# Moving weight conversion behind the recurrence's own work in the first seven steps of a gated-linear-attention and FFN kernel

## The chip, the cores and the metric

One core of a Trainium2 chip. The core has TensorE (PE, matrix products), VectorE (DVE), ScalarE (ACT), GpSimd (POOL) and SyncE (SP, which issues most DMAs). Each runs its own list of instructions in order, and they wait for one another through semaphores. The metric is device time of one execution in microseconds (us), as the median of runs.

## The reference

A recurrent attention block feeds a feed-forward block. The attention inputs q, k, v and alpha have shape (4, 8, 768, 48): batch, heads, sequence, head width.

```python
state = np.zeros((B, H, D, D), dtype=np.float32)
for t in range(S):
    state = alpha[:, :, t, :, None] * state + np.einsum('bhd,bhe->bhde', k[:, :, t], v[:, :, t])
    y[:, :, t] = np.einsum('bhd,bhde->bhe', q[:, :, t], state)
...
x = attn_out.transpose(0, 2, 1, 3).reshape(B * S, H * D)   # 3072 x 384
a = x @ w1          # 384 x 1024
b = x @ w2
h = a * b @ w3      # 1024 x 1024
out = h @ w_out     # 1024 x 384
```

The feed-forward weights arrive as float64; attention inputs and the result are float32.

## The kernel before, in words

**Chunks.** The 3072 tokens are 24 chunks of 128 (four batches of six chunks). Inside a chunk the recurrence is written as matrix products: the logarithm of alpha (`la`, `logs`) is summed along the chunk by a product with a triangular matrix (`decays`, L286, or L289 from chunk 10 on), exponentials of the sums (`e`) scale k and q (`decayed`, L302, on VectorE, tile `qk`), TensorE transposes them (`transposed`, L324; ScalarE copies the result, `qkT`, L326), products of the two give scores (`scores`, L364), and VectorE masks them (`ms`, L367). `attend_state` (L384) and `attend` (L390) make the output from the carried state and from the masked scores; `outer` (L336) adds a chunk's keys and values to the state, with a sum on VectorE (L344, L346); `advance` scales the state on GpSimd every second chunk. The result x is copied by ScalarE (L394) and stored to DRAM (`xd`).

**Weights.** Float64 words are loaded as pairs of 32-bit integers (tile `raw`) and rebuilt as float32 by hand in `to_fp32`. For w1 and w2 there are twelve blocks of 128 x 512, each a generator (`load_gates`) that is taken on in pieces: a fetch issues the block's DMA, and then four calls of `convert(1)` do the rest:

- first: `rest` (L200) and `power` (L205) on ScalarE, two integer operations (L201, L204) on VectorE
- second: three operations on VectorE (L207, L208, L210)
- third: the high part `w` (L217) on ScalarE
- fourth: the low part (L219) on VectorE; for the first six blocks the third part `m` is left to `third`, two products on TensorE (L232, L233) and a copy on ScalarE (L234)

`convert(steps, ahead)` first sees to it that up to `ahead` blocks are fetched.

**Gates.** Groups of three chunks give tiles of 384 tokens. `split_x` splits x into three parts (L412 on ScalarE, L413 and L414 on VectorE), and a gate is 18 products for each of w1 and w2 (L420) over these parts and the weights' parts. Gates of group 0 are put into `fill` in step 6, and `run` takes pieces of them into steps from 7 on, between the attention's own work. After the loop come the remaining gates, the folding of w3 and w_out, and the final products; they are not touched here.

**The loop and its order.** A loop over n = 0 to 24 traces, for each step: stores and loads of later chunks, `attend_state(n - 1)`, `scores(n)`, `transposed(n + 1)`, at n = 6 the first `split_x`, conversion, `advance(n)`, `attend(n - 1)`, `outer(n)`, `third`, gates, conversion, `decayed(n + 2)`, `logs(n + 4)`, conversion, gates, `decays(n + 3)`, conversion, gates. A scheduler turns this into one list for each engine. It goes by the order of tracing and by its own estimates of when things are ready. `after_marks(names)` adds an order: what is traced inside the block comes after the marked instruction, on that instruction's own engine. Marks are `qkT` (ScalarE's copy, L326), `qk` (VectorE's product, L302), `ms` (VectorE's second mask, L367), `e` (ScalarE's second exponential) and `x3` (VectorE's last split of x, L414). The lists are then fixed: an engine whose next instruction waits does nothing else.

SP's queue holds loads of all chunks, the weight blocks and stores of x. Up to eight of its DMAs are outstanding; each issue waits for the DMA eight issues before.

"Chunk c" below is a chunk, "block" a weight block (one to twelve), and "step" is n.

Of the kernel before, what the change touches and what calls it, by code (L numbers as in the profile page):

```python
# [48 lines left out]
def kernel(  # L49
# [18 lines left out]
    N = B * NCH  # L68
# [34 lines left out]
    def bank():  # L103
        return ps.tile([C, 512], FP32, tag="bank", name="bank")
# [3 lines left out]
    def after_marks(*names):  # L108
        stack = ExitStack()
        for x in names:  # L110
            stack.enter_context(tc.issue_after(mark[x]))
        return stack
# [16 lines left out]
    def load_a(n):  # L129
        if n < N:  # L130
            st["a", n] = inp.tile([C, H, D], FP32, tag="ac", name="ac")
            nc.sync.dma_start(out=st["a", n], in_=rows(alpha, n))  # L132

    def load_kq(n):
        if n >= N:
            return
        st["kq", n] = inp.tile([C, 2, H, D], FP32, tag="kq", name="kq")
        nc.sync.dma_start(out=st["kq", n][:, 0], in_=rows(k, n))  # L138
        nc.sync.dma_start(out=st["kq", n][:, 1], in_=rows(q, n))  # L139

    def load_v(n):
        if n < N:
            st["v", n] = vs[n % len(vs)]
            nc.sync.dma_start(out=st["v", n][:, :, 0:D], in_=rows(v, n))
# [91 lines left out]
    def fetch(ahead=3):  # L236
        while weights and len(begun) < ahead:
            begun.append(weights.popleft())
            next(begun[-1])

    def convert(steps, ahead=3):

        for _ in range(steps):
            fetch(ahead)
            if not begun:
                return
            x = begun.popleft()
            try:
                next(x)
                begun.appendleft(x)  # L250
            except StopIteration:
                pass
# [4 lines left out]
    def store():  # L257

        while later:
            dst, src = later.popleft()  # L260
            nc.sync.dma_start(out=dst, in_=src)
# [18 lines left out]
    def decays(n):  # L280
        if n >= N:
            return
        lc = bank()[:, 0:DM]
        la = st.pop(("la", n))
        if n < LATE:
            nc.tensor.matmul(lc, sums[:, n % 2].bitcast(FP32), la, start=True, stop=True)  # L286
        else:
            for i in range(2):
                nc.tensor.matmul(lc, sums[:, n % 2], la[:, i], start=(i == 0), stop=(i == 1))  # L289

        e = st["e", n] = work.tile([C, 2, DM], FP32, tag="e", name="e", bufs=3)
        nc.scalar.activation(e[:, 0], lc, AF.Exp, scale=-1.0)
        mark["e", n] = nc.scalar.activation(e[:, 1], lc, AF.Exp).ins  # L293
        if n in ends:
            nc.gpsimd.dma_start(out=ends[n][0:1], in_=e[0:1, 0])
        if n + 1 in ends:
            nc.gpsimd.dma_start(out=ends[n + 1][1:2], in_=e[C - 1:C, 1])
        load_ends(n)
# [6 lines left out]
    def load_ends(n):  # L305
        if n not in ends:
            return
        with nc.allow_non_contiguous_dma(reason="single values to partitions"):
            for i in range(2):
                nc.gpsimd.dma_start(out=decs[n // 2 % 2][ds(DP * i, D)].rearrange("d m j -> d (m j)"),  # L310
                                    in_=ends[n].rearrange("m (j i d) -> i d (m j)", i=2, d=D)[i])

    def transposed(n):
        if n >= N:
            return
        qk = qks[n % 3]
        qkT = work.tile([C, 2, NP, C], FP32, tag="qkT", name="qkT")

        tp = [bank().rearrange("p (i j c) -> p i j c", i=2, j=NP) for _ in range(2)]
        for i in range(2):  # L320
            for j in range(NP):
                for half in range(2):
                    s = ds(DP * half, DP)
                    nc.tensor.transpose(tp[half][:, i, j, :], qk[s, i, 2 * j:2 * j + 2, :], ident[s, s])  # L324
        for half in range(2):
            mark["qkT", n] = nc.scalar.copy(qkT[:, :, :, ds(DP * half, DP)], tp[half]).ins  # L326
        st["qkT", n] = qkT
# [30 lines left out]
    def scores(n):  # L358
        qkT = st["qkT", n]
        sc = [bank().rearrange("p (j c) -> p j c", j=NP) for _ in range(2)]  # L360
        for j in range(NP):
            for i in range(2):
                r = ds(DP * i, D)
                nc.tensor.matmul(sc[i][:, j, :], qkT[r, 0, j, :], qkT[r, 1, j, :], start=True, stop=True)  # L364
        ms = work.tile([C, 2, NP, C], FP32, tag="ms", name="ms")
        for i in range(2):
            masked = nc.vector.tensor_tensor(ms[:, i].bitcast(I32), sc[i].bitcast(I32), keep_bc, op=ALU.bitwise_and)  # L367
        ends_of_part1[0] = mark["ms", n] = masked.ins
        st["ms", n] = ms
# [3 lines left out]
    def attend_state(n):  # L373
        qkT = st.pop(("qkT", n))

        y = [bank()[:, 0:HP * C].rearrange("p (j c) -> p j c", c=C) for _ in range(2)]
        st["y", n] = y, [(half * HP + j, i, y[i][ds(DP * half, DP), j, :])
                         for j in range(HP) for i in range(2) for half in range(2)]  # L380
        if n % NCH:
            for j, i, to in st["y", n][1]:
                r = ds(DP * i, D)
                nc.tensor.matmul(to, Ts[n % 2][r, j, :], qkT[r, 1, j, :],  # L384
                                 start=(j % HP == 0), stop=False, skip_group_check=True)
# [18 lines left out]
    def load_x(g, queue=nc.sync):  # L404
        st["xT", g] = xp.tile([C, KM, TG], FP32, tag="xT", name="xT")
        queue.dma_start(out=st["xT", g], in_=xd[g].rearrange("(k p) t -> p k t", p=C))

    def split_x(g, i):
        x = st.pop(("xT", g))
        t = tr[i].tile([C, 3, KM, TG], FP32R, tag="x3", name="x3")  # L410
        st["x3", g] = t
        nc.scalar.activation(t[:, 0], x, AF.Copy, scale=1.0 - 2.0 ** -13)  # L412
        nc.vector.tensor_sub(t[:, 1], x, t[:, 0].bitcast(FP32))  # L413
        mark["x3"] = nc.vector.scalar_tensor_tensor(t[:, 2], t[:, 0].bitcast(FP32), -1.0 - 1.0 / P, x,  # L414
                                                    op0=ALU.mult, op1=ALU.add).ins
# [73 lines left out]
    def gate(g, f):  # L489
        yield from (late_gate if late else early_gate)(g, f)  # L490
# [105 lines left out]
    begin = {4 + 4 * g: (g, range(FH if g < 4 else KF)) for g in range(5)}  # L596
    loads = {8: 1, 11: 2, 15: 3, 19: 4}

    for n in range(N + 1):
        store()  # L600
        if n in loads:
            load_x(loads[n])
        load_v(n + AHEAD - 1)
        load_a(n + 5)
        load_kq(n + AHEAD)
        if n:
            attend_state(n - 1)
        if n < N:
            scores(n)
        transposed(n + 1)  # L610
        if n - 2 in begin:
            g, tiles = begin[n - 2]
            with after_marks(("ms", n), ("qkT", n + 1)):
                split_x(g, 0)
            fill.extend(gate(g, f) for f in tiles)
        pieces = (0, 3, 3, 2)[(n - 6) % 4] if n > 5 else 0
        if n == 0:
            with after_marks(("qkT", 0)):
                logs(2)
            decays(2)  # L620
            with after_marks(("e", 2)):
                logs(3)
        early, ready = n < 7, len(thirds)
        behind = after_marks(*[("qkT", n + 1)] * (n < N - 1), *[("qk", n + 1)] * early, *["x3"] * (n - 2 in begin))
        if n < N - 2:
            with behind:
                convert(2 if n == 0 else 1, 2 if n == 0 else 3 if n < 8 else 4)
        advance(n)
        if n:
            attend(n - 1)  # L630
        outer(n)
        third(ready)
        run(pieces > 0)
        if early:
            with after_marks(("qkT", n + 1), ("qk", n + 1)):
                convert(1)
        with after_marks(*[("ms", n)] * (n < 3)):
            decayed(n + 2)
        logs(n + 4)
        if n == 4:  # L640
            load_x(0)
        convert(early and n > 2)
        run(pieces > 1)
        decays(n + 3)
        if n < N - 2:
            convert(early or n % 3 == 0, 3 if n < 8 else 4)
        run(pieces > 2)
        if n == N - 3:
            while begun:
                convert(1)  # L650
            weights.extend(load_out(j) for j in range(KF))
            fetch(4)
# [91 lines left out]
```

## Time and profile before

| | us |
|---|---|
| median of 3 runs (480.33 to 480.93) | 480.89 |
| profiled execution, its own time | 478.61 |
| its span | 476.8 |
| PE busy in the span | 458.3 (96%) |
| DVE busy | 356.3 (75%) |
| ACT busy | 282.1 (59%) |
| POOL busy | 73.1 (15%) |

The span is the time from the first to the last instruction of the profiled execution; its own time has 1.8 us around that. A busy share is an average over stages with different limits. The first 64 us hold steps 0 to 6 and the start of step 7, with PE, DVE, ACT and DMA all at work; later stages are products almost alone. By stretches, PE is busy 3.50 of the first 10 us, 8.06 of the next, then 9.75, 7.36, 9.94, 8.02 and 8.98, and all 10 from 70 to 80 us.

Start times that the text uses, from the trace in order of time:

| | start, us |
|---|---|
| scores (L364) of chunks 1 to 8 | 18.91, 25.41, 31.70, 40.74, 45.71, 50.55, 58.35, 71.4 |
| products qk (L302) of chunks 3 to 8 | 22.78, 33.46, 39.73, 44.34, 50.82, 57.88 |
| raw blocks two, four, five, six landed | 29.38, 37.83, 45.76, 52.48 |
| first gate products (L420) | 64.27 |

### The profile page before, as it was taken

The numbers are of one execution on the slowest core, as the hardware profiler recorded it, in microseconds if no ns is written. First come the engines' busy times: TensorE is split into PE (matmuls) and PEld (weight loads), VectorE is DVE, ScalarE is ACT, GpSimd is POOL, SyncE is SP. The second block draws the span as 40 slices with busy tenths as digits, with TensorE's granted clock in tenths as the row PEclk, the third lists the DMA queues.
The fourth block names the chain that finished last, engine by engine and source line by source line (L and its number), as shares of the span: only waits on it lengthen the run. The fifth ranks groups of instructions, "written<-read, shape, count | busy, mean of one in ns | idle before, by whom it ended". The sixth has DMA issues, their size and how long they took to land.

```text
span 476.8 us, 10002 instructions
## 1 busy us (share of the span) xinstructions
PE 458.3 (96%) x3836; PEld 435.2 (91%) x3836; DVE 356.3 (75%) x576; ACT 282.1 (59%) x556; POOL 73.1 (15%) x140
## 2 busy tenths in 40 slices
PE   4879899999999999999999999999999999999996
PEld 2658589899899999999999999999999999999996
DVE  2769888886988988999998888745642876666761
ACT  4667766866758555898876666644545433333330
POOL 3321231112302310212331101202010100000000
PEclk9888889999999999999999999999999999999999
DMA  9999999999999964657775333122105965555511
GB/s 171 178 200 220 241 211 212 229 234 211 197 216 206 210 202 133 200 170 234 242 216 209 109 124 100 50 84 90 44 36 157 261 189 169 164 170 172 177 51 49
DMA packets 153583, 80.29 MB, mean 168 GB/s; under 512 B 104480, under 2 KB 145568, under 8 KB 153536
## 3 DMA queue, kind: packets, MB, share of 16 engines
q1 hardware_dynamic: 148016, 65.22, 56.8%
q0 software_dynamic: 5520, 14.43, 9.5%
q8 instruction: 30, 0.49, 0.5%
q14 instruction: 17, 0.14, 0.1%
HBM read 57.58 MB, written 22.06 MB: 167 GB/s over the span
## 4 chain that ended last, share of the span: by engine, by line
PE 87%; DMA 5%; SPq 3%; DVE 2%; ACT 1%; issue 1%; DVEq 0%; ACTq 0%
PE bank L420 70%; PE bank L364 5%; PE bank L390 4%; DMA raw<-in_moe_w_dram 4%; PE bank L384 2%; PE bank L324 2%; SPq L139 2%; PE bank L336 1%; PE bank L522 1%; PE bank L289 1%; DMA ac<-in_alpha_dram 1%; SPq L138 1%; SPq L132 1%; PE bank L286 1%; DVE ms L367 0%
## 5 line engine op out<-in xcount | busy, mean ns | idle before, releaser
L420 PE MATMUL bank<-x,w 128*128 128x384 f32 x1152 | 210.9, 337 | 0.0
L420 PEld LDWEIGHTS bank<-x,w 128*128 128x128 f32 x1152 | 200.4, 188 | 1.3 <-issue 0.7
L420 PE MATMUL bank<-w3o,ab 128*128 128x384 f32 x576 | 100.2, 336 | 0.0
L420 PEld LDWEIGHTS bank<-w3o,ab 128*128 128x128 f32 x576 | 99.9, 188 | 0.0
L445 ACT ACTIVATE bank<-bank 128x384 f32<-128x384 f32 x98 | 46.7, 477 | 43.6 <-PE bank L420 43.3
L429 ACT ACTIVATE t<-bank 128x384 f32<-128x384 f32 x62 | 30.6, 494 | 62.3 <-PE bank L420 60.1
L495 POOL DMA_DIRECT2D abd<-ab x46 | 26.9, 584 | 132.8 <-DVE ab L481 125.2
L481 DVE TENSOR_TENSOR ab<-bank,r 128x384 f32<-128x384 f32 x45 | 24.9, 552 | 23.4 <-ACT bank L445 18.6
L551 DVE TENSOR_TENSOR ab<-abl,ab 128x1024 fp32r<-128x1024 f32 x24 | 29.4, 1224 | 13.6 <-ACT ab L550 13.5
L550 ACT ACTIVATE ab<-abl 128x1024 fp32r<-128x1024 f32 x24 | 25.5, 1061 | 20.9 <-PE bank L420 19.2
L326 ACT COPY qkT<-bank 128x512 f32<-128x512 f32 x48 | 26.1, 591 | 19.0 <-PE bank L324 19.0
L367 DVE TENSOR_TENSOR ms<-bank,keep 128x512 int32<-128x512 int32 x48 | 31.4, 683 | 7.8 <-PE bank L364 7.8
L420 PE MATMUL bank<-wo,w3T 128*128 128x384 f32 x192 | 35.9, 334 | 0.0
L420 PEld LDWEIGHTS bank<-wo,w3T 128*128 128x128 f32 x192 | 33.5, 188 | 0.0
L364 PEld LDWEIGHTS bank<-qkT 48*128 48x128 f32 x384 | 25.7, 204 | 7.0 <-issue 4.2
L431 DVE SCALAR_TENSOR_TENSOR o<-bank,t 128x384 f32<-128x384 f32 x24 | 13.4, 557 | 24.0 <-issue 15.6
L364 PE MATMUL bank<-qkT 48*128 48x128 f32 x384 | 30.7, 304 | 0.4 <-ACT qkT L326 0.4
L552 DVE SCALAR_TENSOR_TENSOR ab<-ab,abl 128x1024 fp32r<-128x1024 f32 x24 | 29.2, 1217 | 0.0
L302 DVE TENSOR_TENSOR qk<-kq,e 128x768 f32<-128x768 f32 x24 | 23.0, 958 | 8.2 <-ACT e L293 8.1
L390 PE MATMUL bank<-ms,v 128*64 128x128 f32 x384 | 28.3, 293 | 0.0
L205 ACT ACTIVATE power<-power,rebias 128x512 uint32<-128x512 uint32 (+1 forms) x36 | 25.1, 701 | 4.1 <-DVE power L204 3.8
L200 ACT ACTIVATE rest<-raw 128x512 f32<-128x512 uint32 (+1 forms) x36 | 23.3, 650 | 7.1 <-DMA raw<-in_moe_w_dram 7.1
(80 smaller groups left out, 573.3 us busy)
## 6 DMA issues: line engine op xcount, KB each, us to landing
raw<-in_moe_w_dram SPq DMA_DIRECT2D x28, 512.0 KB, 5.2
abl<-abd SPq DMA_DIRECT2D x24, 512.0 KB, 4.6
abd<-ab POOLq DMA_DIRECT2D x46, 192.0 KB, 3.1
xT<-xd POOLq DMA_DIRECT2D x9, 576.0 KB, 4.5
ac<-in_alpha_dram SPq DMA_DIRECT2D x24, 192.0 KB, 4.7
kq<-in_k_dram SPq DMA_DIRECT2D x24, 192.0 KB, 5.4
kq<-in_q_dram SPq DMA_DIRECT2D x24, 192.0 KB, 4.4
v<-in_v_dram SPq DMA_DIRECT2D x24, 192.0 KB, 5.0
```

The lines of the kernel that those rows point to most:

```text
L205: nc.scalar.activation(power, power, AF.Relu, scale=2.0 ** 23, bias=rebias)
L326: mark["qkT", n] = nc.scalar.copy(qkT[:, :, :, ds(DP * half, DP)], tp[half]).ins
L364: nc.tensor.matmul(sc[i][:, j, :], qkT[r, 0, j, :], qkT[r, 1, j, :], start=True, stop=True)
L367: masked = nc.vector.tensor_tensor(ms[:, i].bitcast(I32), sc[i].bitcast(I32), keep_bc, op=ALU.bitwise_and)
L390: nc.tensor.matmul(to, vc[:, 2 * j + i, :], ms[:, i, j, :], start=(n % NCH == 0 and j % HP == 0), stop=(j % HP == HP - 1), skip_group_chec ...
L420: nc.tensor.matmul(p, w[part][i], x[part][i], start=start and part == parts[0] and i == 0, stop=stop and part == parts[-1] and i == n - 1, ...
L429: nc.scalar.activation(t, p1, AF.Copy, scale=(1.0 + 1.0 / P) * scale)
L445: nc.scalar.activation(p, p, AF.Copy, scale=1.0 + 1.0 / P)
L495: (nc.gpsimd if late else nc.sync).dma_start(out=abd[g][:, f, :], in_=ab)
L550: nc.scalar.activation(t[:, 0], ab, AF.Copy, scale=1.0 - 2.0 ** -13)
L551: nc.vector.tensor_sub(t[:, 1], ab, t[:, 0].bitcast(FP32))
L552: nc.vector.scalar_tensor_tensor(t[:, 2], t[:, 0].bitcast(FP32), -1.0 - 1.0 / P, ab, op0=ALU.mult, op1=ALU.add)
```

## The change

It is in the loop alone. In the first seven steps (`early`), the two places of conversion ahead of `decayed` are put behind one common list of marks: the copy `qkT` of chunk n + 1, the product `qk` of chunk n + 1, and now also the mask `ms` of chunk n (with `x3` in step 6). The first place takes two steps of conversion, the second takes 1, 2, 2, 2, 2, 3, 0; the two later places of conversion take none in these steps. From step 7 on, amounts are as they were. The sums `decays` of chunks 3, 4 and 5, which were traced at the end of steps 0, 1 and 2, are traced after the scores and transposes of steps 1, 2 and 3; `decays(n + 3)` at the end of a step remains from step 3 on.

```diff
         early, ready = n < 7, len(thirds)
-        behind = after_marks(*[("qkT", n + 1)] * (n < N - 1), *[("qk", n + 1)] * early, *["x3"] * (n - 2 in begin))
+        behind = [("qkT", n + 1)] * (n < N - 1) + [("qk", n + 1), ("ms", n)] * early + ["x3"] * (n - 2 in begin)
+        if n in (1, 2, 3):
+            decays(n + 2)
         if n < N - 2:
-            with behind:
-                convert(2 if n == 0 else 1, 2 if n == 0 else 3 if n < 8 else 4)
+            with after_marks(*behind):
+                convert(1 + early, 2 if n == 0 else 3 if n < 8 else 4)
         advance(n)
         if n:
             attend(n - 1)
@@ -632,18 +634,18 @@
         third(ready)
         run(pieces > 0)
         if early:
-            with after_marks(("qkT", n + 1), ("qk", n + 1)):
-                convert(1)
+            with after_marks(*behind):
+                convert((1, 2, 2, 2, 2, 3, 0)[n])
         with after_marks(*[("ms", n)] * (n < 3)):
             decayed(n + 2)
         logs(n + 4)
         if n == 4:
             load_x(0)
-        convert(early and n > 2)
         run(pieces > 1)
-        decays(n + 3)
+        if n > 2:
+            decays(n + 3)
         if n < N - 2:
-            convert(early or n % 3 == 0, 3 if n < 8 else 4)
+            convert(not early and n % 3 == 0, 3 if n < 8 else 4)
         run(pieces > 2)
         if n == N - 3:
             while begun:
```

## The prediction

> **What bounds the kernel now.** I read the slices of the span first, then the chain that ended last, then the start in windows and in order of time.
>
> ```profile
> PE   4879899999999999999999999999999999999996
> DMA  9999999999999964657775333122105965555511
> PEclk9888889999999999999999999999999999999999
> ```
>
> TensorE is at 9 tenths from the sixth slice on (each is 11.9 us), and the chain by engine is 87% PE. So after about 64 us every microsecond is matmul, and the rest of the kernel is as long as its matmuls. Only what happens before the first gate products (L420 at 64.27 us) and the short gaps behind them can move the end. The DMA row says what else is full early.
>
> ```profile
> q1 hardware_dynamic: 35994, 11.27, 104.1%
> ```
>
> That is SP's queue from 8 to 62 us: its packets fill more than the 16 engines' time, at 211 GB/s. Over the span SP's order is the same in both built programs, but for two places: the first xT load (row 49) and the seventh raw block (row 50) trade places, and late in the loop a store trades with a w_out load. Every wait of SP on an engine is met early in both, by the dates below. So the sixth raw weight block lands at about 52.5 us in both versions. The chain shows how that landing reaches the gates:
>
> ```profile
> 46.79 5.69 DMA raw<-in_moe_w_dram
> 52.50 0.43 DVE mant L201
> ...
> 55.71 0.59 ACT w L234
> 56.30 0.43 ACT la L271
> 56.77 1.65 PE bank L286 x2
> 58.42 2.01 PE bank L364 x16
> ...
> 63.77 0.43 PE bank L232
> 64.44 2.64 PE bank L420 x15
> 67.10 0.49 ACT t L429
> ...
> 68.03 0.52 ACT la L275
> 68.59 0.45 PE bank L289
> ```
>
> Two things are to be seen: sums (L286), scores (L364) and the rest stand in a row behind ScalarE's logarithm (la), and TensorE runs at half clock there:
>
> ```profile
> 56.00:57.00 1.00, 0.23 (x1) 0.23 (x2) 0.66 (x2) 1.00 (x3) 0.76 (x2) 0.77 0.83 199
> 57.00:63.00 6.00, 6.00 (x52) 4.81 (x54) 4.10 (x6) 3.85 (x7) 0.67 (x2) 0.50 1.18 265
> 64.00:68.00 4.00, 3.58 (x20) 3.17 (x18) 3.16 (x8) 3.05 (x7) 2.08 (x5) 1.00 0.97 239
> 100.00:180.00 80.00, 79.81 (x1089) 73.51 (x1087) 67.86 (x115) 53.45 (x119) 16.05 (x29) 1.00 0.97 206
> ```
>
> The columns after the window's length are PE, PEld, DVE, ACT and POOL busy; then clock, DMA share and GB/s. PE is idle 1.8 us between 53 and 57, has half clock to 63, and from 72 us on idles 0.4 us in a hundred.
>
> **What the Trainium skill says.** "TensorE: Matmul & The Clock Gate", section "Part 1: The HAM clock gate", has the clock halve after an idle window of some 3.4 us, in free-running windows, and come back after a busy one. The trace agrees in kind: 0.50 for nearly 7 us twice, but each time after only 1.3 to 1.5 us of idle time in the 3.5 us before. "Perfetto Trace Analysis", section "Per-instruction lifecycle", has ScalarE and VectorE strictly first in, first out: what stands behind a waiting instruction waits too. The trace agrees: ScalarE idles 1.13 us at 52.56 for raw block six. "DMA: Bandwidth & Descriptors", section "Specifications", asks for 512 B and more for full rate; here 33,658 of 36,480 packets from 8 to 62 us are smaller, and the queue is full at 211 GB/s.
>
> **The change part by part.** No arithmetic is added or removed. A block takes four steps of conversion, and steps per loop step go from 4,3,3,4,4,4,4 to 3,4,4,4,4,5,2: 26 in both. After step 5 it is 24, six whole blocks, where it was 22. What moves is the order inside each engine, which I read from the two built programs. I date it with starts from the trace.
>
> *Steps 0 to 3.* Sums of chunk 3 no longer stand ahead of scores 1. Those waited for them until 18.07 (la of chunk 3 lands its input at 17.41), so scores 1 start about 16.1, not 18.91. Masks of chunk 2 are no longer behind raw block two (29.38). Scores 3 come near 29, not 31.70, and the product of chunk 4 near 30.2, not 33.46. This gain of 2 to 3 us isn't kept: in the new VectorE order the product of chunk 5 stands behind L201, L204 and L207 of raw block four (landed 37.83): about 40.1, against 39.73. TensorE's transposes of chunk 5 wait for it with part of the attention behind them. I cost these steps at nothing: the full queue hides them. Without that cover they'd be worth the 2 to 3 us.
>
> *Step 5.* Before, ScalarE does la of chunk 8 ahead of block five's w:
>
> ```profile
> 48.49 0.54 ACT L271 ACTIVATE la<-ac 128x384 f32<-128x384 f32 x1
> 49.55 0.63 ACT L217 ACTIVATE w<-mant 128x512 fp32r<-128x512 f32 x1
> 56.19 0.53 ACT L271 ACTIVATE la<-ac 128x384 f32<-128x384 f32 x1
> 56.62 0.62 ACT L217 ACTIVATE w<-mant 128x512 fp32r<-128x512 f32 x1
> ```
>
> After, w comes first both times. It needs VectorE's L210, behind L207, mask, L208, mask: from L207 at 46.6 (block five lands 45.76) four starts of 0.60 bring L210 to 49.0 and its end to 49.7. Then w 0.6, la 0.5: sums of chunk 8 start at 50.8, against 49.21, that is +1.6. Queued behind them on TensorE are the state products and scores 6, with 1.34 between: 52.1 against 50.55. An early scores 5 doesn't help, as block five's landing sets it.
>
> *Step 6.* The masks wait for block six in both (53.91), so scores 6 at 52.1 to 53.2 are in time. On TensorE transposes 0.66, attention 1.03, outer 0.6 and m of block five 0.85 end at 56.3 (55.67 before); ScalarE's m copy 0.5, w 0.6, la 0.5 give sums of chunk 9 at about 57.95, against 56.77: +1.2. Behind those now stands the second product of m of block six (L233, about 0.5 at half clock) ahead of scores 7: 60.05 against 58.35, +1.7.
>
> *Step 7.* TensorE idles as long as before, so I keep the half clock: scores 7 to the end of outer 7 takes 5.35 (58.35 to 63.70), to 65.4. The m products (0.57) that stood here are gone. But VectorE now has the state sum of chunk 7 (L346, 0.3) ahead of the split of x (L413, L414; 1.26 a start, 1.35 long), and L346 needs outer 7. Low part at 67.05, third part at 68.3; with its last three products the first nine end at 68.9. Before nothing waited, and nine products of 0.184 from 64.27 ended at 65.9: +2.9. Against it, TensorE's 1.01 us wait for la at 68.59 falls away, as TensorE is later. The sum: +2.9 - 1.0 = **+1.9 us**.
>
> *The swapped loads.* xT lands at about 60.6 rather than 59.25; ScalarE's L412 now follows transposes 8 anyway (63 to 64), so nothing. Uncovered it would be +1.4. Rest of block seven, ahead of those copies on ScalarE, needs its landing near 59.3 against transposes ending 61 to 63: nothing, and what the lateness exceeds if it lands after them. Later orders differ by single neighbours; with 0.4 us idle in a hundred they are worth 0 +-0.4.
>
> The profiled execution took 478.61 (span 476.8 and 1.8 around it); the sum makes it 480.5. The median of runs shown is 2.28 above that execution, so 482.8.
>
> **Rivals.** Some 0.2% (0.96 us) is what a measurement here can tell from no change.
>
> *Half clock for one window less.* Where windows fall is not set by the kernel. If TensorE regains the clock some 3.4 us earlier in step 7, half of that is saved, +1.9 - 1.7 = +0.2: same, 481.1. For it: at 19 us one window sufficed. Against: the waits for la in steps 5 and 6 leave 1.4 us idle each.
>
> *Faster: the queue lands earlier.* DMA falls to 137 and 140 GB/s in 32 to 34 and 34 to 36 us, with shares of 0.82 and 0.60; at 211 that is 1.4 us lost. If early masks and products remove that dip, blocks four to six land 1.4 sooner. With full clock in step 7 (outer 7 at 62.6, split done 65.6, then la2 by 68.2 against 68.59: -0.4), the sum is -1.8: 479.1. It decides from about 0.6 us of earlier landing. Against it: SP was never short of permitted work in the dip, and bytes and order are the same.
>
> *Much slower.* The wait for the product of chunk 5 (38.8 to 41.1) halves the clock for 6.8 us from about 43: up to +3.4 in steps 4 and 5, of which about 2 reach block six's w through m of block five, queued ahead of it on ScalarE. +4.5: 485.4.
>
> **How the numbers follow.** The forecast's case, +1 to +3.5: 0.50; half clock shorter 0.24; faster 0.16; much slower 0.10. The forecast is 482.8. The range cuts about a tenth below, at 479.6 inside the faster case, and half of the much slower case above, at 485.4; the forecast's own is 481.9 to 484.4. Slower: 0.50 + 0.10 = 0.60; same 0.24; faster 0.16.
>
> **What would show it.** In the changed profile: scores 1 near 16 and scores 3 near 29; raw block six still taken at about 52.5; la of chunks 8 and 9 after w, near 50.3 and 57.4; scores 6 and 7 near 52 and 60; half clock around 57 to 63; L420 stalled for L413 and L414; first L289 near 70.5 instead of 68.59, and the same distance from there to the end. Wrong if block six lands more than 0.6 us earlier, if the clock is full in step 7, or if new waits of ScalarE or VectorE show up in the gates beyond 72 us.

## The result, and the profile after

The changed kernel takes 481.38 us (median of 22 runs, 479.59 to 484.70) where the kernel before, run in turns with it on the same chip, takes 480.17. The ratio is 1.0042, with a 95% interval of 1.0026 to 1.0057: about 2.0 us slower. The two medians lie only 1.2 us apart, at the lower end of that interval, and the two means 1.9, so the size is not known to better than 1.2 to 2.7 us. The prediction was +1.9 us, 482.8 against the 480.89 shown; that the forecast itself lies 1.4 above the measured median is half because before came out at 480.17 over more executions. So direction and size came out, but not by the way that the prediction gave for them, and most of what follows is about that.

The profiled execution took 482.57 us, its span is 480.8 (476.8 before). It lies 1.2 above its kernel's median, where the one of before lay 2.3 below the median shown with it. So 4.0 us lie between these two profiles, twice what the ratio says, and their dates are compared with that in mind.

The slices of the span, changed kernel:

```profile
PE   4978779999999999999999999999999999999996
PEclk9999879999999999999999999999999999999999
DMA  9999999999899983657776343022104965555511
```

Each slice is 12.0 us. PE has 8, 7, 7 in slices four to six, where it had 9, 8, 9, and nines from the seventh on: the loss lies ahead of 72 us. The clock falls in slices five and six alone (two to six before). SP's queue from 8 to 62 us (packets, MB, share of 16 engines):

```profile
q1 hardware_dynamic: 34490, 10.94, 98.5%
```

It is full again, a little less so. Block six was taken by ScalarE at 53.16 (52.56 before). The windows, with the columns as before (length, PE, PEld, DVE, ACT, POOL, then clock, DMA share, GB/s):

```profile
56.00:57.00 1.00, 1.00 (x16) 0.55 (x12) 1.00 (x3) 0.12 (x1) 0.05 (x1) 1.00 1.36 205
57.00:63.00 6.00, 4.65 (x69) 3.62 (x68) 3.20 (x6) 4.17 (x9) 1.35 (x2) 1.00 0.99 244
63.00:64.00 1.00, 0.00 (x0) 0.00 (x0) 0.26 (x1) 0.65 (x2) 0.00 (x0) 1.00 1.21 157
64.00:68.00 4.00, 2.13 (x6) 1.33 (x7) 3.08 (x3) 1.73 (x4) 2.69 (x5) 0.70 0.84 155
100.00:180.00 80.00, 79.44 (x1029) 72.95 (x1029) 68.50 (x117) 52.35 (x117) 15.90 (x30) 1.00 0.98 210
```

Here the picture is turned round. From 57 to 63 us the clock is full (0.50 before), and then TensorE does nothing at all for the microsecond from 63 to 64 and half of the time from 64 to 68. TensorE in order of time says what it waited for (start, length, operation, in brackets the idle time ahead and what ended it):

```profile
50.26 0.91 PE L286 MATMUL bank<-la,sums 128*128 128x384 f32 x2 [1.93 <-ACT la L271]
...
59.72 1.16 PE L364 MATMUL bank<-qkT 48*128 48x128 f32 x16
...
62.23 0.62 PE L336 MATMUL bank<-v,qk 128*64 128x48 f32 x16
64.94 0.80 PE L420 MATMUL bank<-x,w 128*128 128x384 f32 x3 [2.08 <-ACT x L412]
66.33 1.33 PE L420 MATMUL bank<-x,w 128*128 128x384 f32 x3 [0.60 <-DVE x L413]
68.00 4.18 PE L420 MATMUL bank<-x,w 128*128 128x384 f32 x12 [0.34 <-DVE x L414]
71.98 0.52 PE L289 MATMUL bank<-la,sums 128*128 128x384 f32 x1
```

Outer products of chunk 7 (L336) end at 62.85. The first gate (L420), which waited for nothing before, now waits three times, for each of the three parts of x: 3.0 us together. And its last twelve products take 4.18 us, at half clock, which lasts from 65.64 to 72.46 in this execution. The chain that ended last goes through the same place:

```profile
46.78 4.21 DMA kq<-in_q_dram
...
51.02 0.97 DVE qk L302
51.99 1.50 SPq L138
...
55.06 0.83 SPq L192
...
56.00 7.70 DMA xT<-xd
...
63.72 1.17 ACT x L412
...
64.92 1.36 DVE x L413
66.28 1.59 DVE x L414
...
68.00 4.18 PE bank L420 x12
```

Where before had block six and ScalarE's logarithm, there is now SP's queue, block seven's issue (L192) and behind it the load of xT, which takes 7.70 us to land (5.3 before, issued at 53.93). ScalarE's order is as predicted:

```profile
49.16 0.63 ACT L217 ACTIVATE w<-mant 128x512 fp32r<-128x512 f32 x1 [0.44 <-DVE mant L210]
49.70 0.51 ACT L271 ACTIVATE la<-ac 128x384 f32<-128x384 f32 x1
...
57.55 0.63 ACT L217 ACTIVATE w<-mant 128x512 fp32r<-128x512 f32 x1
58.08 0.52 ACT L271 ACTIVATE la<-ac 128x384 f32<-128x384 f32 x1
...
61.73 0.69 ACT L200 ACTIVATE rest<-raw 128x512 f32<-128x512 uint32 x1 [0.77 <-DMA raw<-in_moe_w_dram]
62.32 1.06 ACT L326 COPY qkT<-bank 128x512 f32<-128x512 f32 x2
63.72 1.16 ACT L412 ACTIVATE x<-xT 128x1152 fp32r<-128x1152 f32 x1 [0.35 <-DMA xT<-xd]
```

Both logarithms stand behind `w`, and both are late. L412, the first part of x, is 4.4 us later than in the kernel before, where ScalarE took it ahead of the copies and of block seven:

```profile
59.27 1.16 ACT L412 ACTIVATE x<-xT 128x1152 fp32r<-128x1152 f32 x1
61.37 1.07 ACT L326 COPY qkT<-bank 128x512 f32<-128x512 f32 x2 [0.93 <-PE bank L324]
62.33 0.69 ACT L200 ACTIVATE rest<-raw 128x512 f32<-128x512 uint32 x1
```

Two things hold it back now, and they come within 0.35 us of each other. ScalarE waits for block seven with L200 (landed at 61.64) and then does the copies, to 63.38; and xT itself lands at 63.70.

So the profile offers two causes, and doesn't choose between them: the late logarithms (which the prediction charged with the loss), and the late xT, with what stands ahead of its first reader (which it costed at nothing).

### The profile page after: what moved, and what is told of

It reads as the page before. It is cut to its first block, busy times and chain, and to the rows that moved or that the text cites. A ratio compares the mean times of both kernels' runs of the same rounds, so it can differ in the third digit from the quotient of the medians.

```text
span 480.8 us, 10005 instructions
## 1 busy us (share of the span) xinstructions
PE 459.8 (96%) x3836; PEld 435.3 (91%) x3836; DVE 356.9 (74%) x576; ACT 282.3 (59%) x556; POOL 72.5 (15%) x140
## 4 chain that ended last, share of the span: by engine, by line
PE 86%; DMA 7%; DVE 3%; SPq 1%; ACT 1%; issue 1%; DVEq 0%
PE bank L420 69%; PE bank L364 4%; PE bank L390 4%; DMA raw<-in_moe_w_dram 2%; PE bank L324 2%; DMA ac<-in_alpha_dram 2%; PE bank L384 2%; DMA xT<-xd 2%; PE bank L522 1%; PE bank L336 1%; PE bank L286 1%; PE bank L289 1%; DMA kq<-in_q_dram 1%; DVE qk L302 1%; SPq L139 1%
## 5 line engine op out<-in xcount | busy, mean ns | idle before, releaser
L420 PE MATMUL bank<-x,w 128*128 128x384 f32 x1152 | 214.0, 340 | 3.0 <-ACT x L412 2.1
L420 PEld LDWEIGHTS bank<-x,w 128*128 128x128 f32 x1152 | 202.3, 190 | 5.3 <-ACT x L412 2.2
L420 PE MATMUL bank<-w3o,ab 128*128 128x384 f32 x576 | 100.2, 336 | 0.0
L420 PEld LDWEIGHTS bank<-w3o,ab 128*128 128x128 f32 x576 | 99.9, 188 | 0.0
L420 PE MATMUL bank<-wo,w3T 128*128 128x384 f32 x192 | 35.9, 334 | 0.0
L420 PEld LDWEIGHTS bank<-wo,w3T 128*128 128x128 f32 x192 | 33.5, 188 | 0.0
L205 ACT ACTIVATE power<-power,rebias 128x512 uint32<-128x512 uint32 (+1 forms) x36 | 25.0, 698 | 4.2 <-DVE power L204 3.9
L200 ACT ACTIVATE rest<-raw 128x512 f32<-128x512 uint32 (+1 forms) x36 | 23.2, 647 | 6.6 <-DMA raw<-in_moe_w_dram 6.6
```

The costliest lines, as they stand in the source:

```text
L420: nc.tensor.matmul(p, w[part][i], x[part][i], start=start and part == parts[0] and i == 0, stop=stop and part == parts[-1] and i == n - 1, ...
```

## The experiments

Three theories stand against each other. The prediction's (theory A in the expectations) is that of the late logarithms: sums of chunks 8 and 9 late by 1.6 and 1.2 us, and the split of x behind them. Theory B is xT issued behind block seven: it lands later, and its first reader is later. Theory C is the half clock in the gate, whatever started it. Each kernel is either the kernel before with one part of the change, or the change with one part undone. They ran in three batches, each on one chip with its own runs of the kernel before, and the ratios are against those.

### The two halves of the change

e1 is the kernel before with the sums of chunks 3 to 5 moved, e2 the kernel before with the conversion moved (all of the diff but the `decays` lines).

```diff
+        if n in (1, 2, 3):
+            decays(n + 2)
...
-        decays(n + 3)
+        if n > 2:
+            decays(n + 3)
```

> The kernel before with only the sums of chunks 3 to 5 moved behind the next scores; conversion as before. Theory A (la of chunks 8 and 9 behind w is the cost) and theory B (xT behind raw block seven is the cost) both expect no change from before: ratio 0.998 to 1.002, with scores 1 near 16.4 us, la of chunk 8 ahead of w near 48.5, xT landing near 59, first L289 at 68.6 +-1. If this alone costs over 1 us, both fall.

> The kernel before with only the conversion moved; sums as before. Both theories expect the whole loss of the change: ratio 1.003 to 1.006 (+1.5 to +3 us), la of chunk 8 near 50, xT landing after 62 us, TensorE idle 1 to 2 us ahead of the first L420 and half clock after it.

e1: 0.9995 (0.9977 to 1.0013). e2: 1.0024 (1.0007 to 1.0041). The loss is in the moved conversion, if by less than the 1.003 and more that A and B both expected. In e1 xT is issued ahead of block seven, as before. In e2 xT landed at 62.68, and the first gate waited 2.84 us for L412, then took 6.60 us for 18 products that took 3.31 before.

e1's first gate started at 61.66, 2.6 us ahead of before's, in one profile, and nothing came of it. Its windows say where it went, with two of the kernel before below:

```profile
90.00:100.00 10.00, 8.35 (x90) 7.01 (x83) 8.95 (x15) 6.21 (x14) 1.05 (x2) 1.00 0.94 244
120.00:130.00 10.00, 9.17 (x109) 7.59 (x106) 8.87 (x15) 6.36 (x14) 2.95 (x5) 1.00 0.96 208
160.00:180.00 20.00, 19.07 (x264) 17.36 (x257) 16.98 (x32) 11.50 (x27) 3.61 (x7) 1.00 0.90 240
```

```profile
90.00:100.00 10.00, 9.77 (x117) 8.64 (x112) 9.98 (x16) 7.32 (x16) 1.53 (x3) 1.00 1.00 226
120.00:130.00 10.00, 9.81 (x126) 8.76 (x125) 10.00 (x17) 7.67 (x19) 3.88 (x5) 1.00 0.95 186
```

In e1 TensorE idles 1.65, 0.83 and 0.93 us in its three stretches. In the kernel before it idles 0.23, 0.19 and none there, with VectorE busy 9.98 and 10.00 of 10 us in the first two.

### The change with one part undone

e3 is the change with xT issued ahead of block seven, as before. This also puts the split on VectorE ahead of the state sum L346, as before; the logarithms stay late. e4 is the change with the logarithms of chunks 8 and 9 ahead of `w`, and xT still behind block seven. e5 does both.

```diff
 (e3)
...
+        if n == 4:
+            load_x(0)
+            behind.append("xT")
...
-        if n == 4:
-            load_x(0)
 (e4)
...
         if early:
+            if n in (4, 5):
+                logs(n + 4)
+                behind.append(("la", n + 4))
             with after_marks(*behind):
...
```

> The change, with the first xT load issued ahead of raw block seven as before (x is then split ahead of the state sum of chunk 7, too). Theory A: the logarithms are still late, sums of chunk 9 near 58.5 and gates from about 63; TensorE is late by what steps 5 and 6 lost, ratio 1.002 to 1.005. Theory B: xT lands near 60, the first L420 follows outer 7 at about 63 with no idle time, first L289 at 67 to 69; ratio 0.997 to 1.001.

> The change, with the logarithms of chunks 8 and 9 put ahead of w of blocks five and six on ScalarE; the load of xT stays behind raw block seven. Theory A: sums of chunk 8 near 49, of chunk 9 near 57; most of the loss is gone: ratio 0.999 to 1.002. Theory B: L420 still waits for xT landing at 62 to 64 and for the split, first L289 near 71: ratio 1.003 to 1.006, whatever la does.

> The change with both: xT loaded ahead of raw block seven, and the logarithms of chunks 8 and 9 ahead of w. Theory B (the late xT is the cost) expects what the load alone gave, ratio 0.998 to 1.002. Theory A (the late logarithms cost as well) expects the step from first gates on 1 to 1.5 us earlier still, state products of step 8 at 69 to 70 us, ratio 0.996 to 0.999. Theory D (what starts earlier is given back in waits for VectorE and ScalarE between 90 and 180 us, as in the two runs whose step 8 came early) expects step 8 early and TensorE idle 1.5 to 3.5 us more there: ratio 0.999 to 1.002.

e3: 1.0003 (0.9985 to 1.0020). e4: 1.0023 (1.0007 to 1.0039). e5: 1.0002 (0.9987 to 1.0017). TensorE of e3 in order of time:

```profile
59.53 0.91 PE L286 MATMUL bank<-la,sums 128*128 128x384 f32 x2
...
63.67 1.53 PE L420 MATMUL bank<-x,w 128*128 128x384 f32 x6
65.78 2.33 PE L420 MATMUL bank<-x,w 128*128 128x384 f32 x12 [0.57 <-ACT t L429]
```

Sums of chunk 9 are later still than in the changed kernel (59.53 against 58.65), and yet the gate doesn't wait for L412, waits 0.3 us for L413, and runs at full clock. In e4 sums of chunk 9 come at 57.80, and the gate waits 1.15, 0.60 and 0.57 us for the three parts of x: the wait moved with xT, not with the logarithms. That speaks for theory B. It isn't proof: e3's and e4's intervals overlap, and e3 changes VectorE's order too. Nor did either forecast for e4 come out whole: its ratio lies between the two, and L289 started at 67.98, not near 71. Its profile has the lost time later, with TensorE idle for 1.28 and 1.05 us from 90 to 100 and from 120 to 130.

### One cause alone, in the kernel before

e6 holds the logarithms of chunks 8 and 9 behind `w` of blocks five and six. e7 issues xT behind block seven; VectorE then takes two of block seven's products (L208, L210) ahead of the split as well.

```diff
 (e6)
...
+        if n in (5, 6):
+            with after_marks("w"):
+                logs(n + 3)
...
-        logs(n + 4)
+        if n not in (4, 5):
+            logs(n + 4)
 (e7)
...
-        if n == 4:
-            load_x(0)
         convert(early and n > 2)
+        if n == 4:
+            with after_marks("raw"):
+                load_x(0)
```

> The kernel before with one thing done: logarithms of chunks 8 and 9 held behind w of blocks five and six on ScalarE. Theory A: sums of chunk 8 at about 50.5 and of chunk 9 at 57.5 to 58.5, ratio 1.002 to 1.004. Theory B: the sums are late by as much, but step 7 has the slack; ratio 0.9985 to 1.0015.

> The kernel before with one thing done: the first xT load held behind raw block seven on SP's queue (VectorE then does block seven's products ahead of the split). Theory B: xT lands at 61 to 63, L420 waits for the split, ratio 1.002 to 1.005. Theory A: no change, 0.9985 to 1.0015.

e6: 0.9986 (0.9976 to 0.9997). e7: 1.0049 (1.0035 to 1.0063), about 2.4 us, as much as the whole change within the intervals. These two intervals are far apart, and they decide for theory B against the logarithms. TensorE of e6:

```profile
56.34 0.91 PE L286 MATMUL bank<-la,sums 128*128 128x384 f32 x2 [1.43 <-ACT la L271]
57.18 1.81 PE L364 MATMUL bank<-qkT 48*128 48x128 f32 x16
62.37 3.31 PE L420 MATMUL bank<-x,w 128*128 128x384 f32 x18
```

Measured from the moment when ScalarE takes the block whose `w` they stand behind, sums of chunk 8 are 1.4 us later than before (block five, taken at 44.88 here and 45.84 before) and those of chunk 9 0.7 us (block six, 51.39 and 52.56). But scores of chunk 7 come 5.79 us after block six in both, and the first gate 10.98 after it, against 11.71. So the delay of the logarithms is used up before it reaches the gate. By the same count the changed kernel has 1.6 and 1.3 us, so e6 is the milder test for chunk 9. e3 is the harder one: there they are late by 1.6 and 2.5 us, scores of chunk 7 by 2.0, and the ratio is 1.0003 (up to 1.0020). TensorE of e7:

```profile
59.20 0.62 PE L336 MATMUL bank<-v,qk 128*64 128x48 f32 x16
...
62.61 0.79 PE L420 MATMUL bank<-x,w 128*128 128x384 f32 x3 [2.13 <-ACT x L412]
64.28 0.79 PE L420 MATMUL bank<-x,w 128*128 128x384 f32 x3 [0.88 <-DVE x L413]
65.64 3.67 PE L420 MATMUL bank<-x,w 128*128 128x384 f32 x12 [0.57 <-DVE x L414]
```

That is the changed kernel's signature, three waits for three parts of x and twelve products at half clock, out of one moved DMA in the kernel before. Not all of the wait is the landing. xT landed at 60.77; ScalarE came to L412 at 61.40, since block seven, which is now there first, put its L200 and L205 ahead of it, and the copies of transposes 8 as well. "Perfetto Trace Analysis" of the Trainium skill, section "Per-instruction lifecycle", says that what stands behind another instruction on ScalarE or VectorE waits for it, and these 0.6 us agree.

The same holds wherever xT is issued second. ScalarE has L200 of block seven and the copies ahead of L412, and in e2, e4, e7, e8 and e12 it comes to L412 from other work without idle time, up to 0.7 us after xT has landed. In the profile of the changed kernel alone it still waits for xT, 0.35 us. Where xT is issued first, L412 stands ahead of both. So what is shown is the cost of the changed place in the queue, with all that the scheduler makes of it. Whether the later landing alone would cost as much, or the order on ScalarE alone, no run here shows. By these dates each would hold L412 to within 0.7 us of where it was.

### The half clock by itself

e8 is the change with six further products of 128 x 512 between the outer products of chunk 7 and the first gate, into a bank that nothing reads, to keep TensorE busy while it waits. It adds work and leaves none out.

```diff
         third(ready)
+        if n == 7:
+            spare = bank()
+            for _ in range(6):
+                nc.tensor.matmul(spare, signs[:, 0], w12[0][:, 0, 0, 0, :], start=True, stop=True)
```

> The change with six products of 128 x 512 that nobody reads, put between outer 7 and the first gate products, so that TensorE works in place of waiting for xT (about 2 us at full clock). If the half clock behind the idle time is part of the loss (theory C): no half clock between 64 and 75, first L289 at 70 to 71 instead of 72.0, ratio 1.001 to 1.003. If the wait for xT alone is: the same time as the change, ratio 1.003 to 1.006.

e8: 1.0038 (1.0017 to 1.0059). In its profile the clock is full from 56.2 us on, the twelve products take 2.33 us and L289 starts at 69.61; still the ratio is that of the change, within its wide interval. So the half clock isn't shown as a cause of its own, and isn't ruled out: the interval reaches into both forecasts.

The mean granted clock of each execution says more. Every stretch at half clock in the thirteen profiles, but for those that begin in the last 2 us of the span, is 3.4 or 6.8 us long. One window of 3.4 us takes, by estimate, 0.0036 off the mean (half of 3.4 in 477 us), so the mean counts the windows: 0.982 in the profile of before is five, 0.989 in that of the changed kernel three, and that is what their traces have. Of the 21 executions behind the ratio of e12, the change once more (below), 17 have a mean clock of 0.988 or more, and their median is 478.41, next to the 478.35 of the kernel before. The other four, at 0.979 to 0.982, take 482.31 to 483.34. In e7 the ten executions at 0.984 or more have a median of 480.61 and are still 2.2 us slower than before. So in one batch the loss goes with the half clock, in another most of it is there without the lowest clocks, and the mean doesn't say where in the kernel a window fell. How the 2 us divide between the wait for x and the half clock that follows it stays open.

### The wait that falls away, and the change again

The prediction had taken off 1.01 us because TensorE's wait for the logarithm of chunk 10 (L289) would vanish. e10 is the kernel before with the split of that logarithm (L275, L276) ahead of the first gate's copies, e9 the same in e6. e12 is the change again, on the third chip.

```diff
+            mark["la2", n] = nc.scalar.copy(t[:, 0], la).ins
...
-        run(pieces > 0)
+        with after_marks(*[("la2", 10)] * (n == 7)):
+            run(pieces > 0)
```

> The kernel before with logarithms of chunks 8 and 9 behind w, as in the run that was a little faster, and logarithm and split of chunk 10 ahead of the first gate's copies. If both gains add: ratio 0.995 to 0.998, no idle time ahead of the first L289. If they don't: 0.998 to 1.000.

> The kernel before, with ScalarE's logarithm and split of chunk 10 put ahead of the first gate's two copies, as TensorE waits 1.01 us for them at 68.6. If a wait on TensorE past the first gates is worth its length: ratio 0.997 to 0.999. If later waits for VectorE and ScalarE take it back: 0.999 to 1.001.

> The change itself once more, beside the same runs of before as the two below. Theory B (xT behind raw block seven) and the runs so far: ratio 1.003 to 1.006, xT landing at 61 to 64, TensorE idle ahead of the first L420.

e10: 1.0005 (0.9993 to 1.0017). e9: 0.9990 (0.9975 to 1.0004). e12: 1.0026 (1.0005 to 1.0047), below the range that was expected, and its median of all 22 is only 0.2 us above that of before: the loss is in the few executions named above. In e10 the wait is gone, with L289 at 66.37, and the windows show it given back:

```profile
66.00:76.00 10.00, 9.82 (x114) 8.66 (x112) 9.44 (x19) 6.58 (x15) 3.11 (x5) 1.00 1.06 241
90.00:100.00 10.00, 9.26 (x105) 8.25 (x103) 9.37 (x15) 5.73 (x15) 1.54 (x3) 1.00 1.00 234
120.00:130.00 10.00, 9.17 (x112) 8.24 (x111) 9.79 (x16) 6.90 (x17) 3.25 (x5) 1.00 1.10 206
```

TensorE idles 0.74 and 0.83 us in the last two. This is not so in every kernel with an early gate. From the first L289 to the end of the span it is 408.2 us in the kernel before, and 410.2 to 413.3 in e1, e4, e9 and e10. But in e5 and e6, whose first gates started at 62.28 and 62.37, it is 408.3, and TensorE idles hardly more from 72 to 180 us than before (0.46 and 0.51 us, against 0.42). So the profile of e5 did not bear out theory D, that an early step 8 is given back, though its ratio lies in that theory's range. What decides between the two stays open. None of the eleven runs beats the kernel before by more than the 0.2% that can be told; e6, at 0.14% less, is the nearest.

### All runs by the order of two loads

The first of the pair xT and block seven is issued in the same slot of SP's order in every kernel. From the start of that slot to the landing of xT:

| kernel | xT issued | slot to xT landed, us | ratio |
|---|---|---|---|
| before | first | 5.3 | 1 |
| e1 | first | 5.0 | 0.9995 |
| e3 | first | 5.9 | 1.0003 |
| e5 | first | 5.8 | 1.0002 |
| e6 | first | 6.0 | 0.9986 |
| e9 | first | 5.4 | 0.9990 |
| e10 | first | 4.9 | 1.0005 |
| changed kernel | second | 8.6 | 1.0042 |
| e12 (the same) | second | 7.6 | 1.0026 |
| e2 | second | 8.2 | 1.0024 |
| e4 | second | 8.2 | 1.0023 |
| e7 | second | 8.5 | 1.0049 |
| e8 | second | 8.1 | 1.0038 |

The two groups don't touch in either column: 5.5 us on average against 8.2, and ratios up to 1.0005 against 1.0023 and more, though the intervals of neighbours overlap (e3 up to 1.0020, e12 from 1.0005).

## Why the prediction was right, and where it was wrong

- **What bounds the kernel: right.** The queue is full to 62 us, and block six was taken at 53.16 where 52.5 was said. In the profiles of all the kernels that date lies between 50.95 and 53.23, also among kernels with one and the same early order, so no earlier landing can be read from single profiles. The rival "the queue lands earlier" found no support: e1 gives 0.9995, and the change is slower.
- **Steps 0 to 3: right.** Scores of chunk 1 at 16.38 (16.1 predicted, 18.91 before), scores of chunk 3 at 29.82 (29), product of chunk 5 at 40.10 (40.1). That these gains are worth nothing is what e1 measured, for those of the moved sums.
- **Step 5 and step 6: dates right, worth wrong.** Sums of chunk 8 at 50.26 (50.8), scores 6 at 51.70 (52.1), sums of chunk 9 at 58.65 (57.95), scores 7 at 59.72 (60.05); of the last two 0.6 is the later block six. But the prediction carried these delays into the end, and e6 and e3 show that they cost nothing that can be told (0.9986 and 1.0003) where xT is issued first.
- **Step 7: wrong in its parts.** The clock was to be half from 57 to 63 us; it was full there, and the outer products ended at 62.85 instead of 65.4. L346, which was to hold up the split, was done at 63.26, before ScalarE had even begun L412. The gates' waits for L413 and L414 came as said, but the first and longest is for L412, 2.08 us. The wait at L289 did fall away, as said, and L289 started at 71.98 (70.5 predicted).
- **The swapped loads: this is the step that failed.** "ScalarE's L412 now follows transposes 8 anyway (63 to 64), so nothing. Uncovered it would be +1.4." On ScalarE the copies did end in that range, at 63.38. What had made them harmless was TensorE: at half clock it was to reach the gate only at 65.4, after L412. At full clock it was there at 62.85, and L412 ended at 64.88. And the size was short: the 1.4 was the difference of two landings in one profile, where changing places cost xT 2.7 us (8.2 less 5.5). xT landed at 63.70, where 60.6 was said, and block seven, put near 59.3, at 61.64. Alone this step measures about 2.4 us (e7), so it is large enough for the whole loss.
- **The rivals.** The half clock was not shorter, as one rival had it, but later: 6.8 us of it, in the gate. Much slower by half clock from 43 us didn't happen: the clock fell from 52.0 to 55.4 instead. The prediction had named "the clock is full in step 7" as what would make it wrong. It was full, and the time was met all the same, since the wait for L412, which was put at nothing, took the place of the time that the half clock was to cost. That +1.9 agrees with +2.0 is luck.
- **Beyond 72 us: right for this kernel.** TensorE idles 0.56 us from 100 to 180 us, against 0.19. From the start of L289 to the end of the span it is 408.8 us, against 408.2. For a gain it held in e5 and e6 (408.3) and not in e1 and e10 (413.3 and 410.2).

## What to carry to other kernels

When two neighbours in a full DMA queue change places, price the later one at all that is now ahead of it, here 512 KB or 2.7 us, and follow it to the first instruction that reads it, and to what now stands ahead of that one on its own engine. Don't cost such an edit at nothing on account of cover that exists only while TensorE is at half clock: what removes the half clock uncovers the load. And before a late operation is charged with a loss, make it late alone in the kernel before, by as much as the change does: here it was late by 1.4 and 0.7 us and cost nothing.

## What was unexpected of the hardware

"TensorE: Matmul & The Clock Gate" of the Trainium skill, section "Part 1: The HAM clock gate", speaks of an idle window of some 3.4 us ahead of the half clock. In these profiles less was enough, and the measurement decides (in e7 TensorE was still busy 1.58 of the 3.46 us ahead of the fall): after gaps of 2.13 and 0.88 us in e7 the clock was half from 65.16 to 68.58, and after one of 2.08 us in the changed kernel from 65.64 to 72.46, one and two windows of 3.4 us. It comes late: the products that ran at half clock are those behind the wait, at a time when TensorE had work again. And it moves between executions. The same changed kernel had it at 52.0 to 55.4 and 65.6 to 72.5 in one profile, and at 25.1 to 28.5 and 66.1 to 69.5 in the other, and the profile of before, from which 57 to 63 was taken, was just one such sample.
